# Moving 92 DMA issues from SyncE's queue to ScalarE's, and reading block registers for four slots at once

## The chip, the cores and the metric

The kernel runs on one core of one Trainium2 chip. The metric is the device time of one execution, in microseconds. Of the kernel before there are three such times, and one execution more that the hardware profiler recorded.

## The reference

The kernel computes a block-sparse attention and then a two-layer MLP on its output, all in float32.

```python
# q, k, v: (4, 8, 768, 64); 24 blocks of 32 rows; 3 sampled key blocks for each query block
scores = 1/sqrt(64) * q @ k.T
mask = |blk_i - blk_j| <= 1 | blk_i in (0, 23) | blk_j in (0, 23) | blk_j in sampled_blocks[blk_i]
attn = softmax(where(mask, scores, -1e9));  x = attn @ v            # x as (3072, 512)
h = x @ w_in;  r = max(h, 0);  out = (s * r*r + b) @ w_out          # w_in (512, 2048), w_out (2048, 512)
```

The weights, s and b come as 64-bit floats and are turned into float32 on the chip. Products that need it are made from high and low parts of the operands, three products for one.

## The kernel before

**Attention** is cut into 52 slots, in an order that a string gives. Eight slots are dense ("d"): the first and the last query block of a batch row, which see all keys. Forty-four are sparse ("s"): one inner query block of 32 rows, for two batch rows (e = 0 or 1 names the pair) and all eight heads at once. Three streams A, B and C of consecutive query blocks take turns, so that a stream keeps its window of three neighbouring value blocks and only loads one new block for each slot.

For each slot TensorE runs a fixed chain: the transposes of the exponentials (`t`, L978), the transpose of the slot before's output (second half of `xs`, L1033), the scores of the slot two ahead (`s`, L924 for sparse, L902 for dense slots) and the product with the values (`xs`, "AV", L1021 sparse, L1010 dense). VectorE masks and takes the maximum (L941), scales the output (L1027) and copies half of the transposes out of PSUM (L989). ScalarE takes four exponentials per sparse slot (L953), copies the other half of the transposes (L991), and copies the finished output `xs` to a buffer `xst` in SBUF (`x_copy`, L1038). `xs` has one PSUM bank, so the next slot's AV waits for this copy; `xst` has three buffers.

**SyncE (SP) issues all DMAs.** For a sparse slot these are:
- the new value block of the window into tile `vA` (`window_v`, L753), which waits until the AV of the same stream's slot before has read the old one;
- three sampled value blocks into one of five rows of `vA`/`vB` (`sampled_v`, L846), at addresses taken from registers; where a row changes from e = 0 to e = 1, block 23 as well (L843);
- the spill of the finished output, `xst` to `xd` in DRAM (`spill`, L1045; dense slots L1049);
- every four slots of a stream, four loads of 128 KB that bring the queries of the next four (`load_q`, L700, tiles `qr_0s` to `qr_5s`); the tile is one of four buffers. Dense slots have theirs (`qr_0d`).

The registers are filled by loads from the index tile `vidx` (`block_register`, L822), once for two slots of a stream (RG = 2), on SP for the values and on GpSimd for the sampled keys, which that engine copies (L863, L872, L874).

**What sets the order.** A planner (`Plan`) is given every operation with a cost, a priority, its dependencies and the buffers that it takes, lists them by priority, and writes out one order for each engine. Each queue then runs strictly in that order. Every DMA raises one of eight semaphores, taken in turn by all DMAs of the program, whichever engine issues them; an issue waits until the DMA that used its semaphore eight issues before has landed.

**The MLP** starts inside the same plan. Raw weights are loaded (L57) and decoded by VectorE and ScalarE; the attention output is loaded back from `xd` (`xload`, L386, four loads), split in a high part by ScalarE (L399) and a low part by VectorE (L401), and 30 sub-steps (L468 to L470) follow. Raw weights and raw x share three buffers (`kraw`). After that comes a written-out order of products (L605 and others) that the change does not touch.

Of the kernel before, what the change touches and what calls it, by code (L numbers as in the profile page):

```python
# [98 lines left out]
class Plan:  # L99
# [15 lines left out]
    def op(self, eng, cost, prio, fn, deps=(), alloc=(), use=(), order=(), nbytes=0, cols=0, late=0.0):  # L115


        o = Plan.Op()
        o.cost, o.prio, o.fn, o.nbytes, o.cols, o.late = cost if isinstance(cost, dict) else {eng: cost}, prio, fn, nbytes, cols, late
        o.pick = isinstance(cost, dict)  # L120
        o.deps, o.order, o.alloc = [d for d in deps if d], [d for d in order if d], alloc
        o.end, o.seq = None, len(self.ops)
        for k in (*alloc, *use):
            self.users.setdefault(k, []).append(o)
        self.ops.append(o)
        return o
# [76 lines left out]
def kernel(  # L203
# [16 lines left out]
    nc = tc.nc  # L220
    B, S, DM = v.shape
# [3 lines left out]
    NB = 24  # L225
    BLK = 32
    NPAIR = 4
    NSP = 5
    NSL = 3
    SW = 256  # L230
    STREAMS, LENGTHS = (1, 9, 17), (8, 8, 6)
    NST, KG, VG, RG = 3, 4, 5, 2
    NM = 12
    KP = 4
    NCH = S // P
# [413 lines left out]
    with ExitStack() as es:  # L649
# [38 lines left out]
        qts = {}  # L688
# [5 lines left out]
        def load_q(key, a, par):  # L694
            kind, e, t = key
            if key not in qts:
                qts[key] = qp.tile([P, 2, NPAIR, P], F32, tag="qr", name=f"qr{e}_{t}{kind}")
            rows, b = slice(par * D, (par + 1) * D), 2 * e + a
            src = q_dup[b, t, rows, par::2, :] if kind == "s" and t < NSP else q_edge[b, int(kind == "d"), rows, par::2, :]
            nc.sync.dma_start(out=qts[key][rows, a], in_=src)  # L700

        vbox = {}

# [6 lines left out]
        def value_tiles():  # L710
            if "A" not in vbox:
                for z in "AB":
                    vbox[z] = gp.tile([P, 4, 2, DM], F32, tag="vg", name=f"v{z}", bufs=2)
# [21 lines left out]
        def runs(k, entire):  # L735

            out_, js = [], range(k - 1, k + 2) if entire else (k + 1,)
            for j in js:
                if out_ and out_[-1][1] + out_[-1][2] == j % 3:
                    out_[-1][2] += 1  # L740
                else:
                    out_.append([j, j % 3, 1])
            return out_

        def window_v(i, entire, m):

# [293 lines left out]
        def spill(i):  # L1040
            kind, b, k, _ = slots[i]
            xst = xst_of.pop(i)
            if kind == "s":
                hf, m = divmod(k - 1, NM)
                nc.sync.dma_start(out=xd[2 * b:2 * b + 2, hf, :, m].rearrange("a p c n -> p a (c n)"), in_=xst)  # L1045
                return
            x = k
            for m in range(2):
                nc.sync.dma_start(out=xd[b, 1, :, NM - 2 + m, 2 * x:2 * x + 2, :],  # L1049
                                  in_=xst.rearrange("p x (a m n) -> p (x a) m n", a=2, m=2)[:, :, m, :])  # L1050
# [51 lines left out]


        pq = pdv = pvl = pvs = pk = o_m = o_e = o_rc = o_ev = None
        spills, tensor, lqs, before = {}, {}, {}, {}

        costs = {"s": (530, 470, 265), "d": (810, 350, 780)}
        cols = {"s": (1800, 1024, 500), "d": (1536, 768, 768)}
        for i, (kind, e, k, r) in enumerate(slots):
# [4 lines left out]
            if qk not in lqs:  # L1114
                lqs[qk] = {}
                for a in range(2):
                    for par in range(2):
                        fresh = not (a or par)
                        pq = op("s", 450, max(u - T["QL"], -18.0 if dense else -4.5) + 0.01 * par + (9.5 * (u == 0) if dense else 0.02) * a, lambda qk=qk, a=a, par=par: load_q(qk, a, par),
                                alloc=[("qr", qk)] if fresh else [], use=[] if fresh else [("qr", qk)], order=[pq], nbytes=131e3)  # L1120
                        lqs[qk].setdefault(a, []).append(pq)
            lv, av_deps, av_use, s_deps, s_use = {}, [], [], [], [("qr", qk)]
            if dense:
                for pr in range(2):
                    new = [] if pdv else [("z0", "dv"), ("z1", "dv")]
                    pdv = lv[pr] = op("s", 450, u + pr - T["DL"], lambda i=i, pr=pr: load_v(i, pr), alloc=[("dv", (i, pr)), *new],
                                      use=[] if new else [("z0", "dv"), ("z1", "dv")], order=[pdv], nbytes=393e3)
                av_use = [("z0", "dv"), ("z1", "dv")]
                s_use.append((f"kt{e // 2}", e // 2))
            else:  # L1130
                prev = before.get(r)
                entire = k == STREAMS[r]
                first = not before
                blocks = [*range(k - 1, k + 2), 0] if entire else [k + 1]
                new = [("kk", "kk")] if first else []
                pk = op("g", 1900 if entire else 430, u - T["GK"], lambda i=i, w=entire: window_k(i, w),
                        [*parts_of(e, blocks), *(prev[0] if prev else [])], alloc=new, use=[(f"kt{e}", e)] + ([] if first else [("kk", "kk")]), order=[pk])
                s_deps.append(pk)
                for a in range(NSL):
                    pk = op("g", 430 if a else 700, u - T["GK"] + 0.1 * (a + 1), lambda i=i, a=a: sampled_k(i, a), [o_si, *parts_of(e, range(NB))],  # L1140
                            alloc=[] if a else [("kg", i)], use=[(f"kt{e}", e), ("kk", "kk")] + ([("kg", i)] if a else []), order=[pk])
                    s_deps.append(pk)
                s_use += [("kk", "kk"), ("kg", i)]

                vt = [("vg", "vA"), ("vg", "vB")]
                for m in range(len(runs(k, entire)) + entire):
                    pvl = op("s", 450, u - T["VL"] + 0.1 * m, lambda i=i, w=entire, m=m: window_v(i, w, m), prev[1] if prev else [],
                             alloc=vt if first and not m else [], use=[] if first and not m else vt, order=[pvl], nbytes=131e3)
                    av_deps.append(pvl)
                for a in range(NSL):  # L1150
                    pvs = op("s", 510 if a else 800, u - T["GV"] + 0.1 * a, lambda i=i, a=a: sampled_v(i, a), [o_si],
                             alloc=[] if a else [("vs", i)], use=[*vt, *([("vs", i)] if a else [])], order=[pvs], nbytes=131e3)
                    av_deps.append(pvs)
                av_use = [*vt, ("vs", i)]
# [51 lines left out]
            xc = op("v", 300 if dense else 430, u + T["XA"], lambda i=i: x_scale(i), [a_ops[-1], o_rc], alloc=[("xss", i)], use=[("o", i), ("rc", i)])  # L1206
            tr = op("p", 160 if dense else 230, u, lambda i=i: x_transpose(i), [xc], cols=256 if dense else 512, use=[("xss", i), ("o", i)])
            ac = op("a", 280 if dense else 390, u + T["XA"], lambda i=i: x_copy(i), [tr], alloc=[("xst", i)], use=[("o", i)])
            spills[i] = op("s", 900 if dense else 450, u + T["SPP"], lambda i=i: spill(i), [ac], use=[("xst", i)], nbytes=66e3 if dense else 131e3)
            tensor[i] = s_ops, t_ops, a_ops, tr  # L1210
            if not dense:
                before[r] = s_ops, a_ops[-1:]
# [248 lines left out]
```

## Time and profile before

| | |
|---|---|
| times of three executions | 814.71, 820.22, 821.16 us (median 820.22) |
| time of the profiled execution, its span | 814.4 us, 812.6 us |
| TensorE busy | 738.8 us (91%) |
| VectorE busy | 578.1 us (71%) |
| ScalarE busy | 471.2 us (58%) |
| GpSimd busy | 211.9 us (26%) |
| DMA | 95.67 MB, mean 118 GB/s |

The attention takes the first 276 us of the span, the MLP the rest. Busy time of an engine counts computing instructions only. An issue of a DMA is no busy time, though the queue cannot do anything else meanwhile; how long each took is seen in the timeline of that queue (SPq, ACTq). The wait of an instruction is named by what ended it.

### The profile page before, as it was taken

Reading aid. Unit: us, or ns where it says so; the run is one execution under the profiler, and the core shown is the slowest. Engines: PE = TensorE matmul, PEld = TensorE weight load, DVE = VectorE, ACT = ScalarE, POOL = GpSimd, SP = SyncE. Lnnn points to the kernel's source line nnn. Section 1 sums busy time; section 2 is a strip of 40 time slices with the busy share of each in tenths; the row PEclk is TensorE's granted clock in tenths of the full one; section 3 lists DMA queues with packets and bytes.
Section 4 is the critical chain, followed back from the end, with each engine's and each line's share of the span. In section 5 each row is a group of like instructions: output and inputs, shape, how many; then the busy total and the mean of one; then the engine's idle time right before and its main releaser. Section 6 shows DMA issues by size and latency. Waiting matters only on the chain.

```text
span 812.6 us, 20753 instructions
## 1 busy us (share of the span) xinstructions
PE 738.8 (91%) x7872; PEld 626.2 (77%) x7872; DVE 578.1 (71%) x1439; ACT 471.2 (58%) x1141; POOL 211.9 (26%) x344
## 2 busy tenths in 40 slices
PE   6949888876978599999989999999999999999997
PEld 5737656564656499888977899898889988889996
DVE  3636557654656899999889768778767869766662
ACT  3636557753766777777975344367445547544542
POOL 4422322222322022222002232223223223322321
PEclk9888889998899989999999999999999999999999
DMA  9767797886667533454453323124200012000002
GB/s 277 206 159 208 214 239 199 215 230 180 171 182 197 172 116 108 156 177 137 140 132 122 87 78 102 41 62 122 58 0 1 2 40 64 35 1 1 1 0 79
DMA packets 129636, 95.67 MB, mean 118 GB/s; under 512 B 50304, under 2 KB 109824, under 8 KB 129536
## 3 DMA queue, kind: packets, MB, share of 16 engines
q1 hardware_dynamic: 129536, 94.35, 41.0%
q8 instruction: 62, 1.02, 0.5%
q14 instruction: 38, 0.31, 0.1%
HBM read 75.44 MB, written 14.68 MB: 111 GB/s over the span
## 4 chain that ended last, share of the span: by engine, by line
PE 64%; DVE 16%; DMA 6%; ACT 6%; SPq 4%; issue 3%; ACTq 0%; DVEq 0%
PE m L605 19%; PE o L469 8%; PE o L470 8%; PE o L468 8%; PE t L978 6%; PE xs L1021 5%; PE s L924 4%; DMA vA<-in_v_dram 2%; DVE wkhp L84 2%; DVE win L85 1%; DVE hid L438 1%; DVE wklp L78 1%; DVE ptile L941 1%; PE xs L1010 1%; PE xs L1033 1%
## 5 line engine op out<-in xcount | busy, mean ns | idle before, releaser
L447 POOL TENSOR_TENSOR hid<-hid,hid 128x384 fp32r<-128x384 f32 x120 | 133.2, 1111 | 413.4 <-ACT hid L623 252.3
L622 ACT ACTIVATE hid<-hid,sb_b,sb_s 128x384 f32<-128x384 f32 x96 | 68.0, 709 | 151.9 <-DVE hid L616 151.9
L953 ACT ACTIVATE ptile<-ptile,nm 128x256 f32<-128x256 f32 (+1 forms) x208 | 107.4, 518 | 47.7 <-DVE nm L941 46.8
L941 DVE CUSTOM_DVE_ANT_1 ptile<-s,mt 128x256 f32<-128x256 f32 x176 | 64.3, 421 | 38.2 <-PE s L924 38.0
L1021 PE MATMUL xs<-vA,pt 128*32 128x64 f32 x1696 | 51.4, 233 | 40.4 <-DMA vA<-in_v_dram 16.3
L1021 PEld LDWEIGHTS xs<-vA,pt 128*32 128x32 f32 x1696 | 38.8, 117 | 61.4 <-ACT ptile L953 22.9
L978 PE MATMUL t<-ident,ptile 128*128 128x128 f32 x448 | 67.7, 299 | 0.4 <-ACT ptile L953 0.2
L469 PE MATMUL o<-woutr,hid 128*128 128x512 f32 x168 | 67.2, 400 | 0.7 <-DVE woutr L85 0.7
L468 PE MATMUL o<-woutr,hid 128*128 128x512 f32 x168 | 65.9, 392 | 1.4 <-DVE woutr L83 1.4
L470 PE MATMUL o<-woutr,hid 128*128 128x512 f32 x168 | 67.0, 399 | 0.0
L605 PE MATMUL m<-wout,win 128*128 128x384 f32 x264 | 62.0, 339 | 0.6 <-ACT xrest L1354 0.6
L469 PE MATMUL o<-win,hid 128*128 128x512 f32 x144 | 58.1, 403 | 1.0 <-DVE win L85 1.0
L978 PEld LDWEIGHTS t<-ident,ptile 128*128 128x128 f32 x448 | 53.4, 152 | 7.0 <-ACT ptile L953 1.8
L605 PE MATMUL m<-xp,wop 128*128 128x384 f32 x288 | 58.3, 337 | 0.0
L605 PE MATMUL m<-xp,win 128*128 128x384 f32 x288 | 55.7, 340 | 1.4 <-DVE xp L589 0.7
L616 DVE SCALAR_TENSOR_TENSOR hid<-hid 128x384 f32<-128x384 f32 x96 | 54.3, 566 | 3.3
L605 PEld LDWEIGHTS m<-xp,win 128*128 128x128 f32 x288 | 51.4, 189 | 4.5 <-DVE xp L589 1.2
L874 POOL COPY kk<-kt 128x256 f32 x132 | 48.1, 403 | 21.9 <-issue 21.0
L863 POOL COPY kk<-kt 128x256 f32<-128x256 f32 (+2 forms) x48 | 20.7, 436 | 126.8 <-PE s L924 126.8
L468 PE MATMUL o<-win,hid 128*128 128x512 f32 x126 | 50.6, 401 | 3.5 <-DVE win L83 3.3
L623 ACT CAST hid<-hid 128x384 fp32r<-128x384 f32 x96 | 49.4, 514 | 7.2
L605 PEld LDWEIGHTS m<-xp,wop 128*128 128x128 f32 x288 | 51.5, 188 | 2.1
(166 smaller groups left out, 1784.1 us busy)
## 6 DMA issues: line engine op xcount, KB each, us to landing
vB<-in_v_dram SPq DMA_DIRECT2D x113, 128.0 KB, 3.1
vA<-in_v_dram SPq DMA_DIRECT2D x77, 128.0 KB, 3.7
raw_i<-in_w_in_dram SPq DMA_DIRECT2D x16, 512.0 KB, 3.8
raw_o<-in_w_out_dram SPq DMA_DIRECT2D x16, 512.0 KB, 3.7
vz<-in_v_dram SPq DMA_DIRECT2D x16, 384.0 KB, 4.9
xd<-xst SPq DMA_DIRECT2D x44, 128.0 KB, 2.8
out_dram<-ob SPq DMA_DIRECT2D x20, 256.0 KB, 2.1
sum<-xd SPq DMA_DIRECT2D x12, 384.0 KB, 3.8
```

The lines of the kernel that those rows point to most:

```text
L447: (eng or nc.vector).tensor_tensor(out=htile(5 + i % 3), in0=t, in1=gh.bitcast(F32), op=ALU.subtract)
L468: nc.tensor.matmul(acc, gh[:, tsl], wout(f, 0), start=first, stop=False)
L469: nc.tensor.matmul(acc, gh[:, tsl], wout(f, 1), start=False, stop=False)
L470: nc.tensor.matmul(acc, gl[:, tsl], wout(f, 0), start=False, stop=last)
L605: nc.tensor.matmul(to, w_, x_, start=(c == 0 and k == 0), stop=(c == 1 and k == 2))
L616: vec.scalar_tensor_tensor(out=t, in0=t, scalar=0.0, in1=t, op0=ALU.max, op1=ALU.mult)
L622: nc.scalar.activation(t, t, AF.Identity, bias=sb_b, scale=sb_s)
L623: nc.scalar.copy(gh, t)
L941: nc.vector.tensor_tensor_reduce(out=pt, in0=sp, in1=msk, scale=-scale, scalar=FMAX if g == 0 else nm[:, 0:1], op0=ALU.add, op1=ALU.min, a ...
L953: nc.scalar.activation(pt[:, :w], pt[:, :w], AF.Exp, bias=nms[n][:, last:last + 1], scale=-1.0, accum_out=dns[i][:, g, j:j + 1])
L978: nc.tensor.transpose(tp[:, (2 * j + c) * P:(2 * j + c + 1) * P], src[:, c * P:(c + 1) * P], ident)
L1021: nc.tensor.matmul(xs[quads[pair]], pt[:, c, quads[pair]], vt[:, a, col:col + D], start=(j == 0 and c == 0), stop=(c == 1), tile_position= ...
```

## The change

1. The spills of sparse slots (44 DMAs) and the loads of sparse slots' queries (48 DMAs, twelve groups of four) are issued from ScalarE's queue. Spills and queries of dense slots stay on SyncE. In the plan the moved operations belong to engine "a", with costs of 450 and 500.
2. RG goes from 2 to 4, so that registers for four slots of a stream are read by one load: 12 loads instead of 22, on SyncE and on GpSimd each.
3. A new function, `global_values`, loads the value blocks 0 and 23 of batch rows 0 and 1 for all streams and four ring rows with four broadcasting DMAs, and one more DMA fills the fifth row. These five stand for three loads of block 0 and five of block 23. The bytes written are the same.

```diff
@@ -229,7 +229,7 @@
     NSL = 3
     SW = 256
     STREAMS, LENGTHS = (1, 9, 17), (8, 8, 6)
-    NST, KG, VG, RG = 3, 4, 5, 2
+    NST, KG, VG, RG = 3, 4, 5, 4
     NM = 12
     KP = 4
     NCH = S // P
@@ -697,7 +697,7 @@
                 qts[key] = qp.tile([P, 2, NPAIR, P], F32, tag="qr", name=f"qr{e}_{t}{kind}")
             rows, b = slice(par * D, (par + 1) * D), 2 * e + a
             src = q_dup[b, t, rows, par::2, :] if kind == "s" and t < NSP else q_edge[b, int(kind == "d"), rows, par::2, :]
-            nc.sync.dma_start(out=qts[key][rows, a], in_=src)
+            (nc.scalar if kind == "s" else nc.sync).dma_start(out=qts[key][rows, a], in_=src)
 
         vbox = {}
 
@@ -741,6 +741,18 @@
                 else:
                     out_.append([j, j % 3, 1])
             return out_
+
+        def global_values(m):
+
+
+            value_tiles()
+            if m < 4:
+                z, a = "AB"[m // 2], m % 2
+                n, j = (NST, 0) if z == "A" else (4, NB - 1)
+                nc.sync.dma_start(out=vbox[z][NSL * BLK:, :n, a, :], in_=v[a, j * BLK:(j + 1) * BLK, :].unsqueeze(1).broadcast_to([BLK, n, DM]))
+            else:
+                nc.sync.dma_start(out=sampled_values(0)[NSL * BLK:], in_=block_rows(0, NB - 1))
+                holds["v"].update((row, 0) for row in range(VG))
 
         def window_v(i, entire, m):
 
@@ -1042,7 +1054,7 @@
             xst = xst_of.pop(i)
             if kind == "s":
                 hf, m = divmod(k - 1, NM)
-                nc.sync.dma_start(out=xd[2 * b:2 * b + 2, hf, :, m].rearrange("a p c n -> p a (c n)"), in_=xst)
+                nc.scalar.dma_start(out=xd[2 * b:2 * b + 2, hf, :, m].rearrange("a p c n -> p a (c n)"), in_=xst)
                 return
             x = k
             for m in range(2):
@@ -1102,7 +1114,7 @@
 
 
         pq = pdv = pvl = pvs = pk = o_m = o_e = o_rc = o_ev = None
-        spills, tensor, lqs, before = {}, {}, {}, {}
+        spills, tensor, lqs, before, globs = {}, {}, {}, {}, []
 
         costs = {"s": (530, 470, 265), "d": (810, 350, 780)}
         cols = {"s": (1800, 1024, 500), "d": (1536, 768, 768)}
@@ -1116,7 +1128,7 @@
                 for a in range(2):
                     for par in range(2):
                         fresh = not (a or par)
-                        pq = op("s", 450, max(u - T["QL"], -18.0 if dense else -4.5) + 0.01 * par + (9.5 * (u == 0) if dense else 0.02) * a, lambda qk=qk, a=a, par=par: load_q(qk, a, par),
+                        pq = op("s" if dense else "a", 450 if dense else 500, max(u - T["QL"], -18.0 if dense else -4.5) + 0.01 * par + (9.5 * (u == 0) if dense else 0.02) * a, lambda qk=qk, a=a, par=par: load_q(qk, a, par),
                                 alloc=[("qr", qk)] if fresh else [], use=[] if fresh else [("qr", qk)], order=[pq], nbytes=131e3)
                         lqs[qk].setdefault(a, []).append(pq)
             lv, av_deps, av_use, s_deps, s_use = {}, [], [], [], [("qr", qk)]
@@ -1143,9 +1155,15 @@
                 s_use += [("kk", "kk"), ("kg", i)]
 
                 vt = [("vg", "vA"), ("vg", "vB")]
-                for m in range(len(runs(k, entire)) + entire):
+                if first:
+                    for m in range(5):
+                        pvl = op("s", 450, u - T["VL"] - 0.5 + 0.1 * m, lambda m=m: global_values(m), alloc=[] if m else vt, use=vt if m else [],
+                                 order=[pvl], nbytes=(131e3 if m == 4 else 200e3))
+                        globs.append(pvl)
+                av_deps += globs if e == 0 else []
+                for m in range(len(runs(k, entire)) + (entire and e > 0)):
                     pvl = op("s", 450, u - T["VL"] + 0.1 * m, lambda i=i, w=entire, m=m: window_v(i, w, m), prev[1] if prev else [],
-                             alloc=vt if first and not m else [], use=[] if first and not m else vt, order=[pvl], nbytes=131e3)
+                             use=vt, order=[pvl], nbytes=131e3)
                     av_deps.append(pvl)
                 for a in range(NSL):
                     pvs = op("s", 510 if a else 800, u - T["GV"] + 0.1 * a, lambda i=i, a=a: sampled_v(i, a), [o_si],
@@ -1206,7 +1224,7 @@
             xc = op("v", 300 if dense else 430, u + T["XA"], lambda i=i: x_scale(i), [a_ops[-1], o_rc], alloc=[("xss", i)], use=[("o", i), ("rc", i)])
             tr = op("p", 160 if dense else 230, u, lambda i=i: x_transpose(i), [xc], cols=256 if dense else 512, use=[("xss", i), ("o", i)])
             ac = op("a", 280 if dense else 390, u + T["XA"], lambda i=i: x_copy(i), [tr], alloc=[("xst", i)], use=[("o", i)])
-            spills[i] = op("s", 900 if dense else 450, u + T["SPP"], lambda i=i: spill(i), [ac], use=[("xst", i)], nbytes=66e3 if dense else 131e3)
+            spills[i] = op("s" if dense else "a", 900 if dense else 450, u + T["SPP"], lambda i=i: spill(i), [ac], use=[("xst", i)], nbytes=66e3 if dense else 131e3)
             tensor[i] = s_ops, t_ops, a_ops, tr
             if not dense:
                 before[r] = s_ops, a_ops[-1:]
```

All instructions below are listed in program order of one engine. ScalarE before, for two sparse slots in the middle of the attention (`ptile` is the exponentials' tile, `pt` the copied transposes, the number behind a name only tells buffers apart):

```order
L1038 COPY xst_1204<-xs_1125 128x256
L991 COPY pt_0_1217<-t_0_1181 128x512
L953 ACTIVATE ptile_79,dn_1235<-ptile_79,nm_1219 128x256
L953 ACTIVATE ptile_80,dn_1235<-ptile_80,nm_1231 128x256
L953 ACTIVATE ptile_81,dn_1235<-ptile_81,nm_1245 128x256
L953 ACTIVATE ptile_82,dn_1235<-ptile_82,nm_1266 128x256
L1038 COPY xst_1302<-xs_1222 128x256
L991 COPY pt_0_1315<-t_0_1279 128x512
L953 ACTIVATE ptile_83,dn_1333<-ptile_83,nm_1318 128x256
```

ScalarE after, two sparse slots with the queries' load between them (x4 is four issues):

```order
L965 ACTIVATE ptile_83,dn_1395<-ptile_83,nm_1324 128x256
L965 ACTIVATE ptile_84,dn_1395<-ptile_84,nm_1337 128x256
L965 ACTIVATE ptile_85,dn_1395<-ptile_85,nm_1351 128x256
L1050 COPY xst_1421<-xs_1328 128x256
L1057 DMA xd<-xst_1421 128x2x128
L1003 COPY pt_0_1424<-t_0_1397 128x512
L965 ACTIVATE ptile_86,dn_1395<-ptile_86,nm_1364 128x256
L965 ACTIVATE ptile_79,dn_1449<-ptile_79,nm_1434 128x256
L700 DMA qr_3s<-in_q_dup_dram 64x4x128 x4
L1050 COPY xst_1542<-xs_1440 128x256
L1057 DMA xd<-xst_1542 128x2x128
L1003 COPY pt_0_1567<-t_0_1520 128x512
```

The spill now stands between the copy that it needs (`xst`) and the copy of the transposes (`pt`), which the slot's AV needs. A group of four query loads stands between two exponentials and the next `x_copy`.

SyncE before, about two and a half slots, with the semaphores that each row waits for (DMAHW0 to DMAHW7 are the eight of the DMAs; PE is TensorE, Activation is ScalarE; ISA is arithmetic on a register):

```order
L846 DMA vB<-in_v_dram 32x2x512 [waits DMAHW2_49]
L753 DMA vA<-in_v_dram 32x2x512 [waits DMAHW3_49,PE_49]
L846 ISA
L846 DMA vB<-in_v_dram 32x2x512 [waits DMAHW4_49]
L1045 DMA xd<-xst_1863 128x2x128 [waits DMAHW5_49,Activation_49]
L846 ISA
L846 DMA vB<-in_v_dram 32x2x512 [waits DMAHW6_49]
L846 ISA
L846 DMA vB<-in_v_dram 32x2x512 [waits DMAHW7_49]
L753 DMA vA<-in_v_dram 32x2x512 [waits DMAHW0_49,PE_49]
L846 ISA
```

SyncE after, at a like place:

```order
L858 ISA
L858 DMA vB<-in_v_dram 32x2x512 [waits DMAHW0_49]
L858 ISA
L858 DMA vB<-in_v_dram 32x2x512 [waits DMAHW1_49]
L858 ISA
L858 DMA vB<-in_v_dram 32x2x512 [waits DMAHW3_49]
L858 ISA
L858 DMA vB<-in_v_dram 32x2x512 [waits DMAHW4_49,PE_49]
L765 DMA vA<-in_v_dram 32x2x512 [waits DMAHW5_49,PE_49]
L858 ISA
L858 DMA vB<-in_v_dram 32x2x512 [waits DMAHW6_49]
L858 ISA
```

Before, the numbers of the DMA semaphores run on without a gap from row to row. After, they skip some (from 1 to 3): the numbers between belong to DMAs of ScalarE's queue, and a load of SyncE that comes eight issues after a spill waits until that spill has landed.

The loads of the attention's output, SyncE before (names with numbers, `raw` and `xraw` share their buffers):

```order
L846 DMA vB_275<-in_v_dram 32x2x512
L1045 DMA xd_68<-xst31_3815 128x2x128
L700 DMA qr1_1s_3645<-in_q_dup_dram 64x4x128 x3
L386 DMA xraw0_0_3882<-xd_68 128x12x64
L386 DMA xraw0_1_3892<-xd_68 128x12x64
L386 DMA xraw1_0_3906<-xd_68 128x12x64
L1049 DMA xd_68<-xst32_3908 128x2x32 x2
L753 DMA vA_274<-in_v_dram 32x2x512
L846 ISA
```

SyncE after, at the end of the attention's loads:

```order
L858 ISA
L858 DMA vB_267<-in_v_dram 32x2x512
L765 DMA vA_266<-in_v_dram 32x2x512 x2
L386 DMA xraw0_0_5749<-xd_68 128x12x64
L386 DMA xraw0_1_5782<-xd_68 128x12x64
L386 DMA xraw1_0_5803<-xd_68 128x12x64
L386 DMA xraw1_1_5807<-xd_68 128x12x64
L57 DMA raw_o1_5814<-in_w_out_dram 128x1024
```

SyncE after, earlier, at about slots 25 to 28:

```order
L57 DMA raw_i0_2790<-in_w_in_dram 128x4x256
L765 DMA vA_266<-in_v_dram 32x2x512
L855 DMA vB_267<-in_v_dram 32x2x512
L834 TENSOR_LOAD vidx_123
L858 ISA
L858 DMA vB_267<-in_v_dram 32x2x512
L858 ISA
L858 DMA vB_267<-in_v_dram 32x2x512
L858 ISA
L858 DMA vB_267<-in_v_dram 32x2x512
L57 DMA raw_o0_2879<-in_w_out_dram 128x1024
L57 DMA raw_i1_2917<-in_w_in_dram 128x4x256
```

Before, three of the four x loads stand together between loads of sparse slots' values, and the raw weights come later. After, the first three raw weights take the three buffers while attention runs, and the four x loads stand behind the last value load of the attention.

## The prediction

> **What bounds the kernel now.** I read the page's slices first, then the chain of waits.
>
> ```profile
> PE   6949888876978599999989999999999999999997
> DMA  9767797886667533454453323124200012000002
> GB/s 277 206 159 208 214 239 199 215 230 180 171 182 197 172 116 108 156 177 137 140 132 122 87 78 102 41 62 122 58 0 1 2 40 64 35 1 1 1 0 79
> PE 64%; DVE 16%; DMA 6%; ACT 6%; SPq 4%; issue 3%; ACTq 0%; DVEq 0%
> ```
>
> A slice is 20.3 us. From the fifteenth on TensorE is nearly always busy and nothing of the change is there. The first fourteen, the attention, have gaps on TensorE and the DMA engines at 0.5 to 0.9. The chain gives SP's queue and the DMAs together a tenth of the span. So only the attention can gain. I cut it where `x_copy` (L1038) of slots 4, 8, 22, 34 and 51 starts, and put the entry of the MLP and a later stretch behind it:
>
> ```profile
> core 0: us, PE busy (x) PEld busy (x) DVE busy (x) ACT busy (x) POOL busy (x), PEclk, DMA share, GB/s
> 0.00:48.50 48.50, 36.70 (x566) 29.05 (x566) 24.90 (x97) 22.55 (x72) 20.70 (x67) 0.93 0.83 233
> 48.50:73.20 24.70, 16.64 (x402) 12.74 (x409) 9.36 (x38) 11.25 (x40) 4.29 (x12) 0.72 0.60 160
> 73.20:136.60 63.40, 55.81 (x1480) 39.65 (x1472) 40.78 (x168) 40.69 (x140) 17.50 (x48) 0.89 0.80 221
> 136.60:204.50 67.90, 50.18 (x1200) 36.84 (x1184) 38.45 (x157) 38.22 (x127) 19.84 (x53) 0.92 0.79 210
> 204.50:275.50 71.00, 58.34 (x1698) 43.97 (x1698) 47.02 (x190) 50.01 (x167) 16.33 (x44) 0.94 0.65 176
> 48.50:275.50 227.00, 180.97 (x4762) 133.21 (x4762) 135.60 (x551) 140.17 (x470) 57.96 (x157) 0.89 0.73 197
> 276.00:290.00 14.00, 9.09 (x33) 7.32 (x32) 12.54 (x23) 7.93 (x13) 1.22 (x1) 0.76 0.63 201
> 340.00:360.00 20.00, 19.64 (x99) 17.40 (x98) 19.55 (x32) 14.40 (x27) 5.85 (x5) 1.00 0.54 168
> ```
>
> The 47 slots from 48.5 to 275.5 us take 227 us, 4.8 us each. TensorE's busy time is 181 of them, VectorE's 136, ScalarE's 140; none of the three is full in any stage. What a slot takes when nothing is late is seen in one on ScalarE and TensorE:
>
> ```profile
> 94.52 0.51 ACT L953 ACTIVATE ptile<-ptile,nm 128x256 f32<-128x256 f32 x1 [0.55 <-DVE nm L941]
> ...
> 96.51 0.35 ACT L1038 COPY xst<-xs 128x256 f32<-128x256 f32 x1
> 96.76 0.58 ACT L991 COPY pt<-t 128x512 f32<-128x512 f32 x1
> 97.89 0.51 ACT L953 ACTIVATE ptile<-ptile,nm 128x256 f32<-128x256 f32 x1 [0.54 <-DVE nm L941]
> ```
> ```profile
> 97.25 1.10 PE L1021 MATMUL xs<-vA,pt 128*32 128x64 f32 x64
> 98.28 1.09 PE L978 MATMUL t<-ident,ptile 128*128 128x128 f32 x8
> ```
>
> The period is 97.89 − 94.52 = 3.4 us, with ScalarE working 2.8 and idle 0.55. 47 such slots would be 158 us; 69 us of the 227 are lateness. Who is late, in the waits of the first 285 us:
>
> ```profile
> PE xs L1021 <- DMA vA<-in_v_dram: 16.3, 6, 7.6
> ...
> ACT xst L1038 <- DMA xd<-xst: 10.7, 3, 4.7
> ...
> ACT xst L1038 <- DMA vA<-in_v_dram: 8.3, 1, 8.3
> ACT xp L399 <- DMA xraw<-xd: 7.8, 1, 7.8
> ```
>
> AV waits for window values, `x_copy` for an older spill to free its buffer (in the third row one semaphore that the spill shares with a load), a cast of x for its load. Those 43 us are directly on loads and spills; the rest hangs behind them. And SP's queue, which issues all of them:
>
> ```profile
> 97.38 1.74 SPq L846 DMA_DIRECT2D vB<-in_v_dram  x3
> 99.22 0.37 SPq L753 DMA_DIRECT2D vA<-in_v_dram  x1
> ...
> 100.19 0.39 SPq L1045 DMA_DIRECT2D xd<-xst  x1
> ...
> 106.07 3.40 SPq L700 DMA_DIRECT2D qr_5s<-in_q_edge_dram  x3
> ```
>
> It is solid there: from the first row to the last it issues 15 DMAs in 8.7 us, with 0.1 to 0.2 us between one and the next in most cases, register arithmetic included. So the present bound of the attention is SP's queue with the landings behind it.
>
> **The change part by part.**
>
> ```profile
> L1045 SPq DMA_DIRECT2D xd<-xst x44: 360/388/1324, 61.7 to 275.9; - x44
> L700 SPq DMA_DIRECT2D qr_2s<-in_q_dup_dram x8: 544/610/656, 28.1 to 156.3; - x8
> L822 SPq TENSOR_LOAD <-vidx x22: 1264/1283/1597, 21.9 to 250.1; - x22
> DMA to landing us min/median/max: 2.7/3.9/6.0
> ```
>
> (The last row is that of the query loads, L700.) *SP's relief.* 44 spills × 0.39 = 17 us, 48 query issues × 0.61 = 29 us, ten register loads fewer × 1.28 = 13 us, three value issues fewer × 0.37 = 1 us: 60 us of a queue that was full for most of 276. It also loses the wait of each spill for its `x_copy`. At the other end it can gain waits: eight semaphores are taken in turn by all DMAs, so a value load waits for a spill four slots older to land. I take the SP-bound part of the lateness as gone and ask what is late next.
>
> ```profile
> L399 ACT CAST xp<-xraw 128x384 fp32r<-128x384 f32 x8 | 3.9, 514 | 7.8 <-DMA xraw<-xd 7.8
> ```
>
> (The casts of x: eight of 0.51 us.) *ScalarE's load.* A spill there costs 0.39 to issue plus about 0.16 for its wait on the copy just ahead and the hop: 0.55 (bounds 0.36, the shortest issue, and 1.32, the longest). A query load costs 0.6 (0.54 to 0.66). By the new order 36 of the 48 query issues lie behind slot 4, twelve before it. ScalarE's busy time and issues, stage by stage, against the stage:
> - 48.5 to 73.2: 11.25 + 4 spills × 0.55 = 13.5 of 24.7. TensorE has 16.6. Neither fills it; at 90% of TensorE it is 18, a gain of 6.7.
> - 73.2 to 136.6: 40.7 + 14 × 0.55 + 12 × 0.6 = 55.6 of 63.4.
> - 136.6 to 204.5: 38.2 + 8 × 0.55 + 13 × 0.6 − 0.5 for a cast that moves out = 49.9 of 67.9.
> - 204.5 to 275.5: 50.0 + 17 × 0.55 + 11 × 0.6 − 3.4 for the other casts = 62.6 of 71.0.
>
> ScalarE, at 62% so far, becomes the fullest engine. How full can an engine in strict order get? TensorE got to 88% in the second of these stages, to 82% in the fourth; VectorE to 98% at 340 to 360 us, where work is queued up. I take 90%, nearest to the first: 61.8, 55.4 and 69.6 us, gains of 1.6, 12.5 and 1.4. With 6.7 that is 22.2. At 85% the gains are −2.0, 9.2, −2.6 and 6.7, in all 11; at 95% 4.9, 15.4, 5.1 and 6.7, in all 32.
>
> The issue itself delays what stands behind it. Behind the spill is the copy `pt`, behind the queries are exponentials and `x_copy`. In the slot shown exponentials end at 96.5 and are needed by the transposes at 98.28, 1.7 us of slack; `x_copy` ends at 96.9 and the AV that waits for it starts at 97.25, 0.4 us of slack. The spill comes after `x_copy` and costs `pt` its 0.55, a group of queries (2.4 us) overruns the first slack by 0.7. These are in the 90%, not beside it.
>
> *The Trainium skill speaks against the idea.* The SP rows above show issue after issue with no pause. "DMA: Bandwidth & Descriptors" in the Trainium skill, section "Issuing engines are not separate DMA queues", says that DMAs of all issuing engines end on the same 16 DMA engines, and that starting them from several saves only sequencer time, usually small beside the transfer. By that rule the sum would have no gain here; it is a rival below. In this trace sequencer time is not small: a value load takes 0.37 to issue, and 60 us are lifted from one queue.
>
> *The start.* Eight query loads (1.05 MB) go ahead of the first keys' landing, and the five broadcast loads (1.05 MB in place of as much that came one by one) come earlier. At the first slice's 277 GB/s each megabyte is 3.8 us; bounds 0 and 7.6. The queries had to come in the same 48 us anyway (0.83 of the DMA time there is used): I take +2.
>
> *The entry of the MLP.* The four x loads now follow the last value load instead of running beside attention.
>
> ```profile
> xraw<-xd SPq DMA_DIRECT2D x4, 384.0 KB, 5.4
> ```
>
> The first takes 5.4 us to land, then ScalarE casts and VectorE subtracts. VectorE has raw weights to decode meanwhile (12.5 of 14 us busy at 276 to 290 already), and TensorE nothing but the last slots. I take +5; bounds 0, if decoding was the limit, and 10, if the four split one after another.
>
> Sum: −22.2 + 2 + 5 = −15.2. The profiled execution took 814.4 us (812.6 of span), 5.8 under the median of 820.2. Since the profile is the fastest of what was timed, and the measurement is a median, I set the sum against the median: 805.0.
>
> **The rivals.**
>
> *ScalarE stalls in convoys (slower).* Each group of four queries waits on semaphores that SP's value loads hold, and those wait for AV, which waits for ScalarE. Price of a group: issue 2.4 + one landing of 3.9 − slack 1.7 = 4.6; nine groups behind the start 41; each spill delays `pt` by 0.2 beyond its idle time, 9. If in exchange all 43 us of direct waits go, and start and entry cost 7: +14, 834. It breaks even with 3.0 us a group and is 1% slower from 3.9. For it: the landing of queries takes 2.7 to 6.0 us and ScalarE stands idle only 0.55 a slot. Against it: a semaphore comes round after eight DMAs, which at SP's pace above is 8 × 8.7 / 15 = 4.6 us, longer than a median landing.
>
> *The transfers are the limit and SP only follows them.* Then SP's freed time is spent waiting, on landings of spills and loads, and attention stays as it is; start and entry remain: 820 + 7 = 827. For it: DMA share 0.79 and 0.80 in two stages, and the rule above. Against it: 0.60 and 0.65 in the others, and 221 GB/s where the first stage had 233 and a slice 277.
>
> *All fits.* ScalarE is no bound, the pace is that of the transfers: 227 us × 197 GB/s = 44.7 MB, with 1.6 MB of raw weights that move into attention (three tiles of 128 × 1024 words) 46.3, at 240 GB/s, just over the first stage's 233, 193 us, 34 less; with start and entry −27: 793. For it: the slot of 3.4 us. Against it: 2.8 + 0.55 + 0.5 of queries is already more than 3.4 on ScalarE.
>
> **How the numbers follow.** The forecast, 805 with its own range of 795 to 816 (95% and 85%), has 0.45; the convoys 0.22, the transfers 0.17, all fits 0.16. About 1%, 8.2 us, is what a measurement can tell from no change. Faster than 812: seven tenths of the forecast (0.32) and all of the last, 0.48. Slower than 828.4: the convoys (0.20) and the upper end of the transfers (0.04), 0.24. Between: 0.28. The range goes from 790 to 834; it leaves out the half of the convoys above it and the lower part of the last case, less than 2 in 10.
>
> **What would show it.** Right: SP's queue with gaps in the attention, AV's waits for `vA` below half of 16.3, 136.6 to 204.5 shortened most, ScalarE (busy and issues) near 90% there, and an idle stretch of TensorE of about 5 us more at the MLP's entry. The convoys: waits of ScalarE's queue ahead of L700, with AV and transposes waiting for exponentials and `x_copy` more than now. The transfers: the same DMA bytes per us in the stages, and SP waiting on semaphores. I am wrong if ScalarE holds back TensorE at less than 85%, or if the x loads' landing shows longer than 10 us.

## The result and the profile after

The changed kernel takes 844.43 us (median of 4, 841.41 to 846.12) where the kernel before takes 819.64 (median of 4, 814.71 to 821.16): 1.031 times as long, 95% interval 1.027 to 1.036. The forecast was 805, range 790 to 834. It is slower by 25 us. The profiled execution took 843.71 us, with a span of 841.9 against 812.6. One execution of a later run, spread_x, took 1057.88 us at a granted clock of 0.65; its ratio leaves that one out.

The windows of the profile after, cut at the same `x_copy` starts (now L1050; slots 4, 8, 22, 34 and 51), and the MLP's entry:

```profile
core 0: us, PE busy (x) PEld busy (x) DVE busy (x) ACT busy (x) POOL busy (x), PEclk, DMA share, GB/s
0.00:50.20 50.20, 39.02 (x550) 29.84 (x558) 23.07 (x86) 21.95 (x69) 19.32 (x63) 0.83 0.89 222
50.20:73.90 23.70, 17.49 (x432) 13.31 (x424) 10.91 (x49) 11.25 (x40) 5.79 (x17) 0.78 0.63 170
73.90:156.80 82.90, 55.51 (x1480) 41.05 (x1488) 40.78 (x172) 42.46 (x141) 17.41 (x48) 0.88 0.74 202
156.80:223.70 66.90, 49.81 (x1176) 35.84 (x1184) 39.93 (x156) 37.30 (x124) 18.95 (x49) 0.87 0.65 178
223.70:296.70 73.00, 59.31 (x1730) 43.36 (x1726) 45.73 (x191) 51.52 (x165) 17.37 (x48) 0.95 0.59 162
296.70:320.00 23.30, 15.43 (x58) 13.47 (x58) 16.39 (x28) 15.53 (x32) 4.32 (x4) 0.77 0.50 131
```

No stage from slot 8 on got shorter by more than 1.0 us. Slots 8 to 22 take 82.9 us for 63.4, and the last `x_copy` starts at 296.7 for 275.5: 21 us in the attention. From there to the end it is 545.2 us for 537.1: 8 us at and after the MLP's entry. The DMA share fell to 0.65 and 0.59 in the last two stages (0.79 and 0.65 before), so the engines that move the data have more time to spare than before. The waits of the engines in the first 310 us:

```profile
PE xs L1033 <- DMA vA<-in_v_dram: 32.5, 13, 8.1
...
ACT pt L1003 <- ACT xst L1050: 16.5, 37, 0.5
```

AV waits for window values twice as long as before (16.3). The second row is the spill between `x_copy` and the copy of `pt`: 0.45 us, 37 times. And the waits of SyncE's queue, after and then before:

```profile
SPq L858 <- DMA xd<-xst: 26.8, 12, 4.9
SPq L729 <- DMA xd<-xst: 13.3, 3, 7.4
SPq L386 <- DVE wkhp L84: 10.2, 3, 5.1
SPq L765 <- DMA xd<-xst: 8.9, 4, 3.3
```
```profile
SPq L57 <- DVE win L83: 9.4, 3, 4.8
SPq L1045 <- ACT ptile L953: 6.0, 14, 1.3
SPq L1045 <- ACT xst L1038: 5.4, 5, 3.0
```

SyncE, which no longer issues the spills (`xd`), now waits 49 us in the three rows on `xd` until one has landed. Added up over all instructions of its queue from slot 4 to slot 51, DMA issues fell from 148.5 to 94.7 us and idle time rose from 41 to 118; its waits for DMAs to land, the profile's rows for that stretch added up, rose from 4 to 88. Every microsecond taken from the queue came back as waiting, and more. The largest single jam, in the timeline of SyncE's queue (a row that spans a wait holds it):

```profile
85.31 0.45 SPq L683 DMA_DIRECT2D kt<-in_k_blk_dram  x1
85.87 0.85 SPq L765 DMA_DIRECT2D vA<-in_v_dram  x1
86.95 1.78 SPq L858 DMA_DIRECT2D vB<-in_v_dram  x3
88.77 3.55 SPq L683 DMA_DIRECT2D kt<-in_k_blk_dram  x3
92.42 1.64 SPq L765 DMA_DIRECT2D vA<-in_v_dram  x1
94.30 1.35 SPq L858 DMA_DIRECT2D vA<-in_v_dram  x3
95.70 8.22 SPq L729 DMA_DIRECT2D vz<-in_v_dram  x2
104.02 1.76 SPq L765 DMA_DIRECT2D vA<-in_v_dram  x2
```

Four key loads of 768 KB, which went out one by one between 76 and 114 us before, go out within 7 us. A spill that ScalarE's queue issues behind them at 97.05 lands at 103.50. The second of the two `vz` loads (dense values) has the same semaphore as this spill, which stands eight DMAs ahead of it in the program, and waits 7.4 us for it. The window loads behind it go out at 104.

### The profile page after: what moved, and what is told of

Read it like the earlier page. It is cut to its first block, busy times and chain, and to the rows that moved or that the text cites. A ratio compares the mean times of both kernels' runs of the same rounds, so it can differ in the third digit from the quotient of the medians.

```text
span 841.9 us, 20589 instructions
## 1 busy us (share of the span) xinstructions
PE 745.6 (89%) x7872; PEld 630.4 (75%) x7872; DVE 576.7 (69%) x1439; ACT 475.2 (56%) x1141; POOL 212.9 (25%) x344
## 3 DMA queue, kind: packets, MB, share of 16 engines
q10 hardware_dynamic: 25024, 12.06, 5.5%
## 4 chain that ended last, share of the span: by engine, by line
PE 51%; DVE 17%; DMA 7%; ACT 6%; issue 3%; ACTq 1%; SPq 0%; DVEq 0%
PE m L605 18%; PE o L469 8%; PE o L470 7%; PE o L468 7%; DMA vA<-in_v_dram 4%; PE xs L1033 3%; PE t L990 3%; PE s L936 2%; DVE wklp L78 2%; DVE hid L438 1%; DVE wkhp L84 1%; DMA xd<-xst 1%; DVE win L85 1%; DVE wkhp L75 1%; DVE win L83 1%
## 5 line engine op out<-in xcount | busy, mean ns | idle before, releaser
L1033 PE MATMUL xs<-vA,pt 128*32 128x64 f32 x1696 | 50.5, 229 | 44.5 <-DMA vA<-in_v_dram 32.5
L990 PE MATMUL t<-ident,ptile 128*128 128x128 f32 x448 | 69.5, 302 | 12.2 <-ACT ptile L965 10.9
```

The costliest lines, as they stand in the source:

```text
L990: nc.tensor.transpose(tp[:, (2 * j + c) * P:(2 * j + c + 1) * P], src[:, c * P:(c + 1) * P], ident)
L1033: nc.tensor.matmul(xs[quads[pair]], pt[:, c, quads[pair]], vt[:, a, col:col + D], start=(j == 0 and c == 0), stop=(c == 1), tile_position= ...
```

## The experiments

Two theories stood first. *Order*: the planner, told that SyncE has less to do, bunched prefetches, and that jams the transfers. *Queue*: issues from ScalarE's queue, and the waits that they make, cost the time. The first four runs are meant to separate them; all ratios are to the kernel before, run on the same chip. Its median there lies between 819.1 and 819.6 us throughout, so that times of different runs can be set side by side.

**queue_only.** The kernel before in its order, the issues moved:

```diff
-            nc.sync.dma_start(out=qts[key][rows, a], in_=src)
+            (nc.scalar if kind == "s" else nc.sync).dma_start(out=qts[key][rows, a], in_=src)
-                nc.sync.dma_start(out=xd[...], in_=xst)      # sparse spill; the plan still says "s"
+                nc.scalar.dma_start(out=xd[...], in_=xst)
```

> The kernel before with its own order of work (key loads at slots 9, 10, 15 and 16, x loads at slot 30, registers for two slots); only the sparse spills and query loads are issued from ScalarE's queue, at their old place in the program. Theory 'order' (the new order bunches 3 MB of key loads, dense values and raw weights and backs up the transfers): 812 to 825 us, near the kernel before. Theory 'queue' (issues on ScalarE and SyncE's waits for their landings cost the time): 835 us or more, with tens of us of SyncE waiting for spills to land.

827.85 us, 1.010 (1.006 to 1.013), between the two forecasts. **order_only** is the opposite: the changed kernel with both lines put back to `nc.sync`, the plan left at "a".

> The changed kernel with the planner still told that spills and sparse queries belong to ScalarE, so that the order is the new one, but all of them are issued from SyncE's queue. Theory 'order': 838 us or more, with the same jam at slots 9 to 12. Theory 'queue': 820 to 828 us (only the later entry of the MLP remains, about 8 us).

823.14 us, 1.003 (1.000 to 1.006). So the new order alone costs 4 us, next to nothing, and the queue alone about 8 us. Together that is 12 of the 25 us; the other half comes only where both meet. **spread** holds the key loads and the dense values back by order edges in the plan:

```diff
+            copies.append(ac)                       # x_copy of each slot
+        for p, n in enumerate((8, 9, 15, 17)):
+            kld[(1, 0, p)].order.append(copies[n])
-    use=..., order=[pdv], nbytes=393e3)             # dense values
+    use=..., order=[pdv] + ([copies[i - 3]] if i > 20 else []), nbytes=393e3)
```

> The changed kernel, with the four key loads of the second pair held back to slots 10, 11, 17 and 19 and the dense values to three slots ahead, as before; queues as changed. Theory 'order': 12 to 20 us of the 25 are won back, 824 to 832 us, slots 8 to 22 take 63 to 70 us. Theory 'queue': 840 us or more.

845.59 us, 1.033 (1.028 to 1.038). **spread_x** adds `order=list(xl.values())` to the raw weights' loads, so that the x loads come first.

> As 'spread', and the x loads take the raw buffers ahead of the raw weights, at slot 28, as before. Theory 'order': another 8 us less than 'spread', 816 to 824 us, since the MLP's entry is as before. Theory 'queue': about 832 us.

847.58 us, 1.034 (1.029 to 1.040), above both forecasts. The jam at slots 9 to 12 was real, but taking it apart wins nothing: slots 8 to 22 get 5 us shorter (77.6), slots 22 to 34 10 us longer (76.8), both in spread. In order_only the same jam is paid back by itself: it is 26 us behind the kernel before at slot 27 and 3 us at slot 51, presumably since what was loaded early isn't loaded later. "Order" by itself as the cause of the attention's loss falls. "Queue" stands, and for it there were two mechanisms: time that issues take on ScalarE, and the eight landing semaphores that both queues share, the *ring* below.

**queue_spill** and **queue_q** move one kind each, in the order of before.

> The kernel before in its own order, only the 44 sparse spills issued from ScalarE's queue. The run with both moved cost about 8 us. Theory 'shared ring' (each DMA waits for the landing of the one eight before it, so two queues hold each other up and SyncE's freed time turns into waits): no gain, 817 to 825 us, SyncE waiting 20 us or more on landings of spills. Theory 'issue time on ScalarE': also no gain, and ScalarE's exposed issues about 44 x 0.55 = 24 us.

833.03 us, 1.019 (1.014 to 1.023), above both forecasts.

> The kernel before in its own order, only the 48 sparse query loads issued from ScalarE's queue. Shared ring: 820 to 830 us, most of the 8 us that both together cost, because a query load stands where ScalarE's program has it and SyncE may run only seven DMAs past it. Issue time on ScalarE: about half of the 8 us.

826.29 us, 1.009 (1.006 to 1.013). In the order of before, issue time on ScalarE is out as the cost of the spills. There a spill is issued while the copy of `pt` runs, and of 44 x 0.37 us of issues only 0.7 us fell, added up, into time in which ScalarE did nothing else:

```profile
100.46 0.58 ACT L991 COPY pt<-t 128x512 f32<-128x512 f32 x1
100.58 0.39 ACTq L1045 DMA_DIRECT2D xd<-xst  x1
```

For the queries it is not excluded: in queue_q, 6.7 us slower than before, 7.6 of 28.0 us of issues stand beside no computing. In queue_spill nothing but the issuing queue differs from the kernel before, and SyncE's waits in it read:

```profile
SPq L846 <- DMA xd<-xst: 21.1, 11, 3.5
SPq L700 <- DMA xd<-xst: 11.3, 5, 4.5
SPq L729 <- DMA xd<-xst: 5.7, 2, 5.1
```

Before, a spill went out 6.3 us (median) after its `x_copy`, when SyncE came to it; from ScalarE's queue after 0.03 us. The only one that gains by that is an `x_copy` that waits for a spill to free its buffer (10.7 us before, 5.7 in queue_spill).

All waits for landings on SyncE's queue, from slot 4 to 51, come to 4 us before and 74 in queue_only, while its issues fell from 148.5 to 97.6: taken together, the queue has more to do than before.

The ring is that of SyncE and ScalarE only, not of every engine that issues: the traces show their DMAs on the same eight semaphores (numbers 100 to 107) and GpSimd's on eight others (112 to 119 in gp_all). So **gp_spill** and **gp_all** move the same DMAs there (`nc.gpsimd` in the lines of queue_only), in the order of before.

> The kernel before in its own order, the 44 sparse spills issued from GpSimd's queue, whose DMAs have semaphores of their own and do not stand in the ring of eight. Shared ring: the ring then holds loads only; 805 to 815 us, faster than with the spills on ScalarE by 5 us or more. Issue time on ScalarE: no reason to gain against the kernel before, 815 to 825 us; and if the transfers are what limits, the same.

801.51 us, 0.980 (0.976 to 0.984).

> As gp_spill, and the 48 sparse query loads too from GpSimd's queue: 92 DMAs out of the ring. Shared ring: 795 to 812 us. Transfers as the limit: 815 to 825 us, with the DMA engines' share no higher than now. GpSimd's copies of sampled keys may be held up behind the issues; that would show as scores waiting for them.

789.71 us, 0.965 (0.961 to 0.968): 30 us faster than before and 55 us faster than the change, with the same DMAs. Both runs came out faster than was expected of the ring. SyncE's waits for landings are nearly gone (12 us from slot 4 to 51); it waits for the AV that frees a window block:

```profile
SPq L753 <- PE xs L1021: 17.4, 13, 3.8
...
SPq L753 <- PE t L978: 3.9, 4, 1.5
SPq L846 <- DMA kt<-in_k_blk_dram: 3.4, 3, 1.3
SPq L846 <- DMA vA<-in_v_dram: 3.2, 3, 1.8
SPq L846 <- DMA xd<-xst: 2.8, 1, 2.8
```

The stretch from slot 4 to slot 51 takes 202.8 us for 227, and moves 218 GB/s where before it was 197 and after 181:

```profile
47.90:250.70 202.80, 174.82 (x4794) 127.41 (x4787) 136.86 (x562) 140.59 (x471) 111.27 (x241) 0.94 0.79 218
```
```profile
50.20:296.70 246.50, 182.13 (x4794) 133.56 (x4778) 137.35 (x563) 142.53 (x469) 59.52 (x162) 0.89 0.66 181
```

Counted from the issues and landings in these stretches, 4.34 DMAs are in flight on average in the change, 4.36 in queue_only and 6.53 in gp_all. A landing took 3.6, 3.6 and 4.6 us on average: with more in flight each takes longer, and still more arrives. Of the kernel before, half of the landings aren't known; rg4 below, which has its queues and its time, had 4.78 in flight.

But GpSimd's queue differs in more than the ring. The rows of the page on the moved 12.06 MB, of the change and of gp_all (packets, MB, share of 16 engines):

```profile
q10 hardware_dynamic: 25024, 12.06, 5.5%
```
```profile
q0 software_dynamic: 4416, 12.06, 5.1%
```

Its packets are larger. So **gp_all_tiny** puts places back into the ring without the bytes:

```diff
                 nc.gpsimd.dma_start(out=xd[...], in_=xst)
+                nc.scalar.dma_start(out=tiny[i:i + 1, :], in_=xst[0:1, 0, 0:8])
```

> As gp_all (789.7 us), and behind each sparse spill one DMA of 32 bytes from ScalarE's queue, from the same tile to a spare place in DRAM. It moves nothing to speak of, but stands in the ring of eight semaphores as the spill did. Shared ring: 797 to 812 us, with SyncE waiting for these small DMAs to land. If GpSimd's queue is better for another reason (larger packets, no ring needed): 788 to 793 us.

804.27 us, 0.982 (0.976 to 0.988). 44 DMAs of 32 bytes cost 14.6 us. SyncE's waits in it, and the small DMAs themselves:

```profile
SPq L847 <- DMA tiny<-xst: 22.2, 15, 3.4
...
SPq L754 <- DMA tiny<-xst: 6.4, 2, 3.4
```
```profile
L1047 ACTq DMA_DIRECT2D tiny<-xst x44: 200/201/466, 46.6 to 265.8; - x44
```

**gp_all_tiny92** adds another 48 from a constant tile, one at the place of each sparse query load.

> As gp_all (789.7 us), with 92 DMAs of 32 bytes from ScalarE's queue: one behind each sparse spill (as in gp_all_tiny, 804 us) and one for each sparse query load, at its place, reading a constant. If places in the ring of eight are the whole of what GpSimd's queue won, about 812 to 822 us, near the kernel before. If the larger packets of GpSimd's queue (2.7 KB against 0.5 KB) or the transfers' timing hold the rest: 802 to 808 us.

815.25 us, 0.994 (0.991 to 0.997). With all 92 places taken again and no bytes behind them, 25.5 us are lost (789.71 to 815.25) of the 29.9 that gp_all had won over the kernel before. But the run to set this against is queue_only, whose 92 DMAs stand at the same places of the same queue: 827.85, 38.1 us above gp_all. So places in the ring alone hold two thirds of what ScalarE's queue loses to GpSimd's. What the other 12.6 us are, isn't taken apart: the 92 DMAs of queue_only also move bytes, in smaller packets than GpSimd's, and take longer to issue than the small ones (0.37 to 0.6 us for 0.2).

**gp_after** is the changed kernel with `nc.gpsimd` for `nc.scalar`.

> The changed kernel (its order, registers for four slots, the five broadcast loads), with spills and sparse queries issued from GpSimd's queue instead of ScalarE's. Shared ring: the new order alone cost 4 us from SyncE's queue, so 790 to 800 us, with the MLP's entry some 8 us later than in gp_all. If the order is what costs: 810 us or more.

802.01 us, 0.980 (0.975 to 0.986), 2 us above the forecast of the ring: the new order, too, is faster than before once the DMAs stand outside the ring, and it is 12 us slower than the old one there.

**rg4** and **globals** take the two smaller parts alone.

> The kernel before with registers read for four slots at once, nothing else. By the trace after, a load of 12 registers takes 2.54 us where one of 6 took 1.28, so the sum is the same: 815 to 824 us, no difference. By the prediction 13 us of SyncE's queue are saved: 808 to 815 us.

818.97 us, 1.000 (0.997 to 1.004).

> The kernel before with the five broadcast loads of blocks 0 and 23 instead of eight single ones, and the order that the planner then makes; queues and registers as before. 814 to 826 us: three issues fewer against a megabyte that comes earlier. The key loads of the second pair then stand at slots 13 to 16.

820.69 us, 1.002 (0.999 to 1.004). Neither counts. The register loads of SyncE in rg4 (the prediction shows the row of before):

```profile
L822 SPq TENSOR_LOAD <-vidx x12: 1266/2474/2682, 23.8 to 242.0; - x12
```

Ten of the twelve loads have twelve registers, two have six. Added up they take 27.7 us (28.8 in the change), and the 22 of before, of six each, took 29.6. Twelve registers take twice as long as six.

**The MLP's part.** From the last `x_copy` to the end of the span the kernels with the old order (before, queue_only, queue_spill, queue_q, gp_spill, gp_all, both tiny ones, rg4, globals) take 536.8 to 539.2 us, those with the new order (after, order_only, gp_after, spread, spread_x) 542.9 to 545.3, whatever the queue. So 6.5 us on average (544.5 for 538.0), 8 in the change, are the order's, and lie there. In the change TensorE waits at the entry for x:

```profile
299.89 0.69 PE L426 MATMUL h<-xp,win 128*128 128x384 f32 x1 [3.46 <-ACT xp L399]
```

The wait above of the x loads, 10.2 us, is for VectorE to free the raw buffers, which hold weights. With x first (spread_x) TensorE waits for weights instead, and the 8 us stay:

```profile
308.86 0.69 PE L426 MATMUL h<-xp,win 128*128 128x384 f32 x1 [8.30 <-DVE win L83]
...
315.80 0.69 PE L426 MATMUL h<-xp,win 128*128 128x384 f32 x1 [2.19 <-DVE win L83]
```

**What stays open.** Order alone and queue alone make 3.8 and 8.5 us by medians, and the change makes 24.8. One thing that only the two together have is seen in the change: there a spill stands ahead of the copy of `pt`, a group of queries ahead of exponentials, and the computing waits for the issues.

```profile
97.05 0.38 ACTq L1057 DMA_DIRECT2D xd<-xst  x1
97.47 0.59 ACT L1003 COPY pt<-t 128x512 f32<-128x512 f32 x1 [0.45 <-ACT xst L1050]
...
231.29 2.14 ACTq L700 DMA_DIRECT2D qr_3s<-in_q_dup_dram  x2
233.48 0.51 ACT L965 ACTIVATE ptile<-ptile,nm 128x256 f32<-128x256 f32 x1 [2.53 <-issue]
```

From slot 4 to 51, issues beside no computing of ScalarE add up to 34.0 us in the change, against 5.0 in queue_only. So issue time on ScalarE is a rival to the ring for up to half of the loss; gp_after takes both away at once, and no run parts them. (By spans of profiled executions the parts are 11.6 and 15.2 us and the change 29.3. But the profiled execution of before is 5 us under its median, and that stands in each of the three, so twice in the sum of the parts.)

It is open, too, why the same ring makes two queues *slower* than one (1.010 and 1.019 in queue_only and queue_spill), rather than equal. It was only followed in the waits; no run has the same queues with a ring of another size.

## Why the prediction was wrong

- *The bound* was half right. SyncE's queue was solid and landings stood behind it. What was not seen is that the two cover each other: at one issue in 8.7 / 15 = 0.58 us the eighth DMA back has had 4.6 us, about a landing's time. Take issue time away and the same loads wait for landings. The prediction used this very figure, against the convoys, and left the consequence out of the sum.
- **The step that failed** is "I take the SP-bound part of the lateness as gone and ask what is late next". It named the gain of waits on spills in the sentence before, without a price. The runs put that in its place: issues on SyncE fell by 54 us and its idle time rose by 77; waits for landings went from 4 to 88 us, of which 49 are the three rows on spills. AV's waits for `vA`, which were to fall below half of 16.3 us, rose to 32.5.
- *SyncE's relief* was 60 us. As issues it was 54 from slot 4 on, more than the 47 charged, but of the 13 us of register loads there is only 1 (29.6 to 28.8); the term was taken by the count of loads, and the time goes with the count of registers. "Runtime: NRT & Kernel Launch" in the Trainium skill, section "Instruction fetch mechanics", has such a load at about 200 ns a register even in bulk; here 2.54 / 12 = 0.21 us agrees.
- *ScalarE's load* came out close; what was made of it did not. In the four stages 13.5, 55.6, 49.9 and 62.6 us were charged, and busy time with the issues beside no computing measures 12.8, 53.0, 46.1 and 64.7. (A spill held up the copy behind it by 0.45 us, for 0.55 charged: 0.38 of issue and 0.07 of wait and hop, for which 0.16 was charged.) The wrong step is that the engine would fill to 90% and so set the time. It filled to 54, 64, 69 and 89% of the stages, 72% in all: only in the last stage, at 89%, can it have been near a bound. The 22 us gained at 90% had no ground. They also hold a slip: 16.64 us at 90% are 18.5 and not 18, so the first stage's gain was 6.2.
- *The start*: slot 0's `x_copy` is 6.2 us later and slot 4's 1.7; +2 was right. Its reason is only half tested: in order_only, with the queries on SyncE, slot 0 isn't later (−0.2).
- *The entry*: +5 was forecast, bounds 0 to 10, 8 came. The reason given, a landing of 5.4 us, was the smaller part (the first took 5.2): the other loads could not be issued, as raw weights held their buffers. That is not the whole cause either, since with x first the 8 us stay.
- *The convoys* had the sign (834, "slower") and part of the mechanism: waits on semaphores held by the other queue. But it was SyncE that stood, for 77 us more. ScalarE's queue waited some 13 us for landings ahead of the query loads, where nine groups were priced at 3.9 us each, and in the order of before the run with spills alone lost more than that with queries alone.
- *The transfers as the limit* said that SyncE's freed time would be spent waiting, which it was. But not on transfers: gp_all moves the same bytes at a higher rate.
- The rule that was weighed there, "Issuing engines are not separate DMA queues" in "DMA: Bandwidth & Descriptors" of the Trainium skill, would have forecast no gain, and was nearer to the result than the sum. Its ground, that all DMAs run on the same 16 engines, isn't touched by these runs; its conclusion that the choice of queue matters little is: the same 92 DMAs give 0.965, 1.000 or 1.010 by the queue alone.
- The range ended at 834. It was priced with ScalarE's waits only, and had no term for SyncE's.

## What to carry to other kernels

Before DMAs are moved to a second queue, look at what each issue waits for: if all DMAs take turns at a few landing semaphores, two queues hold each other up, and a queue that is "solid with issues" may only be hiding landings. Count DMAs in flight (here 4.3 in the change, 6.5 in gp_all) rather than issue time alone, and try a queue whose DMAs have semaphores of their own; here that gave 789.71 us, 3.5% under the kernel before. When a planner is told a new cost, its whole order moves: run the order and the queue apart.

## What the runs showed of the hardware

- An issue on ScalarE's queue runs beside computing that was started ahead of it (in queue_spill all but 0.7 of 16 us of issues), and holds up the computing that stands behind it (0.45 us, 37 times, behind spills of the change; 2.53 us once behind queries).
- A register load takes 0.21 us per register: 1.28 us for six, 2.47 to 2.54 for twelve.
- The same transfers went in packets of 482 bytes from ScalarE's queue (25024) and 2.7 KB from GpSimd's (4416), at 5.5 and 5.1% of the span of 16 engines.
- With more DMAs in flight a landing takes longer: 3.6 us on average at 4.3, 4.6 at 6.5.
